# Chunk attention and two gated layers on one core: sums of x on VectorE, exponent terms on ScalarE, the low part of g taken last

## The chip, the cores and the metric

The kernel runs on one NeuronCore of a Trainium2 chip. Five engines work side by side, each through its own queue in order: TensorE (PE, matrix products; PEld is its loading of weights), VectorE (DVE), ScalarE (ACT), GpSimd (POOL) and SyncE (SP, which issues most DMAs). An instruction waits only at the head of its own queue, and all that stands behind it waits too. The metric is the device time of one execution in microseconds (us); lower is better.

## The reference

```python
# q, k, v: (4, 8, 576, 64); attention inside chunks of 64 positions
scores = q_c @ k_c.T / 8
attn = exp(scores - max); attn /= sum(attn) + 1e-9
x = (attn @ v_c)  -> (2304, 512)            # tokens x model
g = (x @ w_a) * (x @ w_b)                    # 512 -> 1536
y = g @ w_out                                # 1536 -> 512
h = y @ w_in                                 # 512 -> 2048
P = a0 + a1 h + a2 h^2 + a3 h^3
Q = 1 + |b0||h| + |b1| h^2
out = (P / (Q + 1e-6)) @ w_out2              # 2048 -> 512
```

All inputs are float32. Each matrix product is taken in three parts (high by high, high by low, low by high), so every operand is split into a rounded high part (ACT copies it) and the rest (a subtraction).

## The kernel before

The 2304 tokens are three groups of 768. The program is written in the order in which each engine is to do it; there is no scheduler behind it.

**Stage A** (up to about 197 us of the trace): attention in 18 units of 128 tokens, the first three at once (a list called FIRST), the others between the products x@w_a and x@w_b of the first group, which are taken directly (`ab_half`, 384 tokens at a time). After every six matmuls `half()` emits pieces of other work: the weights' conversion (`w_piece`, four pieces per tile: an ACT and a DVE instruction make the exponent terms, DVE shifts one, ACT writes the mantissa's low part, a DVE instruction adds them, then high and low parts) and whatever a list of due times (`todo`, moved on by `tick`) has due. A unit of attention is seven such entries (transposes of k and q, scores, exp, softmax, transpose, product with v); FROM, PER and GAP set their distances. Scores and the product with v share the PSUM buffers `a` and `b`.

**Sums of x.** For groups 1 and 2 the products use seven products of half matrices instead of eight. `x_first` and `x_second` make the sums and splits of x that this needs: 8 subtractions (L433) and 14 low parts (L415), each 128x768, all on POOL; high parts on ACT (L414). They read two x32 buffers; the next group's copies (L396) wait until a buffer is done with.

**Stage B** (about 197 to 383 us): 24 steps (`s_step`), each with products 1, 2, 5, 6, 4 of its own tile and products 7 (`third`) and 3 (`last`) of the step before. Product 3 adds into the tile q that the DVE instruction at L613 has to read first. `s_prep` makes sums and splits of the weights on DVE and ACT. In `fill()` the pieces of w_out's conversion and the due entries are emitted.

**Stage C** (about 383 to 557 us): y = g @ w_out in five blocks of tokens (256, then four of 512) and 12 tiles each, 60 steps. In each, `g_fetch` brings g back from DRAM two steps ahead, ACT makes its high part (L649), DVE its low part (L651), and `y_part` takes 4 x 3 matmuls into four accumulators, column block by column block. Between them the second layer's weights are converted; their DMAs and those of g stand in one SP queue. g_hi and g_lo have two buffers each.

**Stage D** (from about 552 us): `step2` takes h = y @ w_in, the rational function on ACT and DVE and the last product. Tile (0, 2) of h is the first that uses PSUM buffer `a`.

At the start SP issues the loads of attention and weights, then two tiny ones of the constants a and b; ACT's absolute value of b (L818) stands directly behind FIRST.

Of the kernel before, what the change touches and what calls it, by code (L numbers as in the profile page):

```python
# [15 lines left out]
ALU = mybir.AluOpType  # L16
# [4 lines left out]
def chunk_attention_two_mlps(  # L21
# [176 lines left out]
    def w_piece():  # L198


        n, piece = divmod(n_cv[1], 4)
        n_cv[1] += 1
        key = order[n]
        if piece == 0:
            w_fetch_ahead(n)
            t = raws.pop(key)

            terms[n] = (t, *w_tile(key, I32))
        t, c, z = terms[n]
        hw = t[:, :, 1]  # L210
        lw = t.rearrange("p f t -> p (f t)").bitcast(U16).rearrange("p (f t) -> p f t", t=4)[:, :, 1]
        zz = z.bitcast(F16).rearrange("p (f t) -> p f t", t=2)
        if piece == 0:
            nc.scalar.activation(zz[:, :, 1], hw.bitcast(F32), AF.Copy, scale=2.0 ** -112)
            nc.vector.tensor_scalar(c.bitcast(F32), hw.bitcast(F32), 2.0 ** -112, None, ALU.mult)
        elif piece == 1:
            w_hi(n - 1)
            nc.vector.tensor_scalar(c, c, 3, None, ALU.logical_shift_left)
        elif piece == 2:
            nc.scalar.activation(zz[:, :, 0].bitcast(U16), lw, AF.Copy, scale=2.0 ** -13)  # L220
            w_lo(n - 1)
            w_fetch_ahead(n + 1)
        else:
            del terms[n]
            x = f32s[n] = p_io.tile([P, DM], I32, name="w_x", tag="io")
            nc.vector.tensor_tensor(x, c, z, ALU.add)
            if key in w1_d:
                nc.gpsimd.dma_start(out=w1_d[key], in_=x.bitcast(F32))

    def w_until(tiles):  # L230

        while n_cv[1] < min(4 * tiles, 4 * n_cv[2]):
            w_piece()

    def w_flush():

        n = n_cv[1] // 4 - 1
        if n in f32s:
            w_hi(n)
            w_lo(n)  # L240

    def mm3(ps, w, x, first, last, **kw):
        (wh, wl), (xh, xl) = w, x
        nc.tensor.matmul(ps, wh, xh, start=first, stop=False, **kw)  # L244
        nc.tensor.matmul(ps, wh, xl, start=False, stop=False, **kw)  # L245
        nc.tensor.matmul(ps, wl, xh, start=False, stop=last, **kw)  # L246

    def cols(pair, k):
        return [t[:, k * P:(k + 1) * P] for t in pair]
# [5 lines left out]
    def later(dt, f):  # L255
        todo.append((now[0] + dt, n_todo[0], f))
        n_todo[0] += 1
# [152 lines left out]
    def x_hl(g, c, x):  # L410
        t = x_block(g, c)
        hi, lo = t[:, 0], t[:, 1]
        return (
            lambda: nc.scalar.copy(hi, x),  # L414
            lambda: nc.gpsimd.tensor_tensor(lo, x, hi.bitcast(F32), ALU.subtract),  # L415
        )

    def x_first(g):
# [7 lines left out]
    def x_second(g):  # L426


        x1, x2 = un.pop(("x32", g, 0)), un.pop(("x32", g, 1))
        b11, b21, b12, b22 = x1[:, 0:2], x1[:, 2:4], x2[:, 0:2], x2[:, 2:4]  # L430

        def sub(o, x, y):
            return lambda: nc.gpsimd.tensor_tensor(o, x, y, ALU.subtract)  # L433

        h3, l3 = x_hl(g, 3, b22)
        h5, l5 = x_hl(g, 5, b11)
        h7, l7 = x_hl(g, 7, b12)
        h6, l6 = x_hl(g, 6, b11)
        h4, l4 = x_hl(g, 4, b21)
        for at, f in (  # L440
            (0.5, sub(b11, b12, b11)), (0.5, h3), (0.5, sub(b12, b22, b12)),
            (1.5, l3), (1.5, h5), (2, h7),
            (2, l5), (2.5, sub(b11, b22, b11)),
            (3.5, l7), (3.5, h6), (4, sub(b21, b21, b11)),
            (4.5, l6), (5, h4),
            (5.5, l4),
        ):
            later(at, f)

    def a_unit(u, at, times):  # L450

# [188 lines left out]
    def g_fetch(j, i):  # L640
        t = p_io.tile([P, SIZES[j]], F32, name="g_raw", tag="io")
        nc.sync.dma_start(out=t, in_=g_d[i][:, START[j]:START[j] + SIZES[j]])
        raw["g", j, i] = t
# [7 lines left out]
        return lambda: nc.vector.tensor_tensor(lo, x, hi.bitcast(F32), ALU.subtract)  # L651

    def y_part(j, i):
        if i == 0:
            places = [(ps_acc, "acc")] * KD if j % 2 == 0 else [(ps_at, "at"), (ps_at, "at"), (ps_ab, "a"), (ps_ab, "b")]
            acc[j] = [pool.tile([P, SIZES[j]], F32, name="acc", tag=tag) for pool, tag in places]
        w, g = wt["o", i], g1.pop((j, i))
        for d in range(KD):
            mm3(acc[j][d], cols(w, d), g, i == 0, i == F1 - 1)
            if i == F1 - 1:  # L660
                evac.append(lambda d=d: y_out(j, d))

# [141 lines left out]
    for item in FIRST:  # L804
# [9 lines left out]
        else:  # L814
            {"S": a_scores, "X": a_exp, "E": a_soft, "P": a_ptrans, "V": a_pv, "L": lambda u: un.pop(("lo", u))()}[
                what
            ](u)
    nc.scalar.activation(cb_t, cb_t, AF.Abs)  # L818
    for u in (2 * UH, 2 * UH + 1):
        a_load(u, "k", "q", "v") if u == 2 * UH else a_load(u, "v")  # L820

# [1 line left out]
    seq = [(i, h) for h in range(2) for i in range(4)] + [(i, h) for i in range(4, F1) for h in range(2)]  # L823
    for n in range(UH):
        a_unit(UH + n, 1.0 + 0.5 * n, (0, 0.5, 1.5, 2, 2.5, 3.5, 4.5))
    FROM, PER, GAP = 6.0, 2.75, 1.0
    times = (0, 0.5, 2, 3, 3.5, 5, 6.5)
    for n in range((NQ - 1) * 2 * UH):
        a_unit(2 * UH + n, FROM + PER * n + (GAP if n >= 2 * UH else 0), times)
# [11 lines left out]
    def s_do(t, op):  # L841
        if op == 0:
            preps[t] = s_prep(t)
        preps[t][op]()
        if op == 11 and t + 2 < F1:
            s_load(t + 2)
# [49 lines left out]
    def fill():  # L896
        step, m = place
        place[1] += 1
        for t, op in plan.get((step, m), ()):
            s_do(t, op)  # L900
        if (step, m) == (1, 3):
            w_fetch_ahead(len(order1))
        if step >= 2 and (7 * step + m) % 3 == 0:
            w_until(min(n_cv[1] + 1, 4 * n_cv[2]) / 4)
        tick(0.5)

    for n, (i, g) in enumerate(seq2):
# [2 lines left out]
            g_fetch(0, 0)  # L910
            g_fetch(0, 1)
        prev = s_step(i, g, prev, fill)
    place[:] = [len(seq2), 2]
    s_step(None, None, prev, fill)
    tick(100.0)
    w_until(n_cv[2])
    w_flush()
    g_parts(0, 0)()
    s_t.close()
    phase.close()  # L920
    s_x32.close()
# [10 lines left out]
    done = n_cv[1]  # L932
    a_ring = None
    for n, (j, i) in enumerate(places):
        if n + 2 < len(places):
            g_fetch(*places[n + 2])
        due = done + (4 * len(order2) * spent[n] // spent[-1] if n < len(spent) else 4 * len(order2))
        due -= n_cv[1]
        low = lambda: None
        if n + 1 < len(places):  # L940
            low = g_parts(*places[n + 1])
        if due:
            w_piece()
        low()
        for _ in range(due - 1):
            w_piece()
        y_part(j, i)
        evacuate(1)
        if j == NB - 1:
            if 2 <= i < 2 + KD:  # L950
                y_split(0, i - 2)
            if 1 <= i < 1 + KD:
                y_fetch(0, i - 1)
            if i >= F1 - EARLY:
                if a_ring is None:
                    w_flush()
                    s_cv.close()
                    p_a = ctx.enter_context(tc.tile_pool(name="a", bufs=1, side="right", reuse_waits="tile"))
                    a_ring = p_a.tile([P, AN], F32, name="a_ring", tag="a_ring")
                step2(i - (F1 - EARLY))  # L960
# [32 lines left out]
```

## Time and profile before

| | |
|---|---|
| time, median of 3 runs | 960.22 us (957.68 to 961.83) |
| the profiled execution's time | 956.45 us |
| its span, first to last instruction | 954.7 us |
| PE busy | 909.1 us (95%) |
| PEld, DVE, ACT, POOL busy | 798.4, 745.0, 594.2, 107.0 us |
| granted TensorE clock, mean | 0.977 of full speed |

Matmuls are pipelined, so a busy PE need not be PE at its rate: the count of matmuls in a stretch tells more. In the rows further down a timeline row is: start, duration, engine, line, operation, output<-inputs, shape, count, and in brackets the idle time before it and what ended that. A row of stretches is: the stretch and its length, then busy time and count of each engine, the granted clock, the DMA engines' share and GB/s.

### The profile page before, as it was taken

The page shows a single profiled execution, that of the slowest core. Times are in us where ns is not written, and L with a number is a line of the kernel's source. Part 1 is how long each engine was busy: PE and PEld are TensorE (multiplying, and loading weights), DVE is VectorE, ACT ScalarE, POOL GpSimd, SP SyncE. Part 2 cuts the span into 40 slices and gives each one's busy share as a digit, 9 for nine tenths or more (in the row PEclk, how much of TensorE's full clock was granted, in tenths as well). Part 3 has the DMA queues.
Part 4 walks back from the last instruction along what each step waited for, and adds up shares of the span by engine and source line. Part 5 has one row for each costly group of instructions (what it writes and reads, how often), then busy time and mean ns, then how long its engine had stood idle before and what let it go on. Part 6 is the DMA issues. An engine that isn't in the chain of part 4 may idle for free.

```text
span 954.7 us, 14746 instructions
## 1 busy us (share of the span) xinstructions
PE 909.1 (95%) x5516; PEld 798.4 (84%) x5516; DVE 745.0 (78%) x1334; ACT 594.2 (62%) x1070; POOL 107.0 (11%) x144
## 2 busy tenths in 40 slices
PE   6779998979999999899999899999999999999998
PEld 5669987979999999777777699888888888888897
DVE  5467889596888886466666569999888988988896
ACT  4546766534445453366666568887668767776875
POOL 0111354361111111000000000000000000000000
PEclk8789999979999999899999999999999999999999
DMA  9957996224443323457676520020002002000100
GB/s 230 246 168 202 250 239 162 84 81 138 139 147 133 130 99 109 136 191 246 224 245 213 203 89 1 1 77 1 1 1 89 0 1 76 3 1 1 45 1 34
DMA packets 107335, 105.82 MB, mean 111 GB/s; under 512 B 61440, under 2 KB 84480, under 8 KB 107264
## 3 DMA queue, kind: packets, MB, share of 16 engines
q1 hardware_dynamic: 99264, 79.71, 28.6%
q0 software_dynamic: 8000, 25.17, 7.3%
q8 instruction: 43, 0.70, 0.3%
q14 instruction: 28, 0.23, 0.1%
HBM read 74.98 MB, written 29.88 MB: 110 GB/s over the span
## 4 chain that ended last, share of the span: by engine, by line
PE 74%; DMA 9%; ACT 6%; DVE 5%; SPq 4%; issue 2%; ACTq 0%; DVEq 0%
PE acc L245 8%; PE acc L246 8%; PE acc L244 8%; DMA g_raw<-g_d 7%; PE h L246 7%; PE h L244 7%; PE h L245 7%; PE ab L244 3%; PE ab L246 3%; PE ab L245 3%; PE y L246 3%; PE y L245 3%; PE y L244 3%; SPq L313 2%; PE q L244 2%
## 5 line engine op out<-in xcount | busy, mean ns | idle before, releaser
L246 PE MATMUL h<-y,w_i 128*128 128x512 f32 (+1 forms) x320 | 117.8, 368 | 0.0
L244 PE MATMUL h<-y,w_i 128*128 128x512 f32 (+1 forms) x320 | 117.8, 368 | 0.0
L245 PE MATMUL h<-y,w_i 128*128 128x512 f32 (+1 forms) x320 | 117.7, 368 | 0.0
L716 ACT ACTIVATE a_ring<-h 128x512 f32<-128x512 f32 (+1 forms) x80 | 44.1, 551 | 88.8 <-PE h L246 88.8
L245 PE MATMUL acc<-g_lo,w_o 128*128 128x512 f32 (+1 forms) x240 | 92.7, 386 | 5.4 <-DVE g_lo L651 5.0
L244 PE MATMUL acc<-g_hi,w_o 128*128 128x512 f32 (+1 forms) x240 | 91.7, 382 | 5.0 <-ACT g_hi L649 4.9
L572 ACT COPY s<-y 128x384 f32<-128x384 f32 x72 | 34.5, 479 | 90.5 <-PE y L246 89.3
L246 PE MATMUL acc<-g_hi,w_o 128*128 128x512 f32 (+1 forms) x240 | 90.5, 377 | 0.0
L651 DVE TENSOR_TENSOR g_lo<-g_raw,g_hi 128x512 fp32r<-128x512 f32 (+1 forms) x60 | 38.1, 637 | 54.8 <-ACT g_hi L649 54.7
L719 DVE SCALAR_TENSOR_TENSOR u<-u,cb_t,a_ring 128x512 f32<-128x512 f32 (+1 forms) x80 | 55.7, 696 | 31.3 <-ACT u L717 30.4
L245 PE MATMUL acc<-w_o,g_hi 128*128 128x512 f32 x191 | 75.2, 394 | 0.0
L244 PE MATMUL acc<-w_o,g_hi 128*128 128x512 f32 x191 | 74.8, 392 | 0.0
L246 PE MATMUL acc<-w_o,g_lo 128*128 128x512 f32 x191 | 74.2, 388 | 0.0
L649 ACT CAST g_hi<-g_raw 128x512 fp32r<-128x512 f32 (+1 forms) x60 | 34.5, 575 | 63.2 <-DMA g_raw<-g_d 45.5
L244 PEld LDWEIGHTS h<-y,w_i 128*128 128x128 f32 x320 | 60.1, 188 | 9.0
L245 PEld LDWEIGHTS h<-y,w_i 128*128 128x128 f32 x320 | 60.1, 188 | 8.7
L246 PEld LDWEIGHTS h<-y,w_i 128*128 128x128 f32 x320 | 60.0, 188 | 7.5
L486 POOL DMA_DIRECT2D g_d<-g x72 | 40.6, 565 | 203.4 <-DVE g L616 83.2
L245 PEld LDWEIGHTS acc<-g_lo,w_o 128*128 128x128 f32 x240 | 46.5, 194 | 20.1 <-DVE g_lo L651 12.1
L244 PEld LDWEIGHTS acc<-g_hi,w_o 128*128 128x128 f32 x240 | 46.5, 194 | 17.7 <-ACT g_hi L649 9.6
L718 ACT ACTIVATE t<-h,ca_t 128x512 f32<-128x512 f32 (+1 forms) x80 | 59.0, 738 | 0.0
L721 DVE SCALAR_TENSOR_TENSOR t<-t,ca_t,h 128x512 f32<-128x512 f32 (+1 forms) x80 | 55.6, 694 | 2.8
(193 smaller groups left out, 2522.6 us busy)
## 6 DMA issues: line engine op xcount, KB each, us to landing
w_raw<-in_moe_w_out_dram SPq DMA_DIRECT2D x28, 512.0 KB, 3.8
g_d<-g POOLq DMA_DIRECT2D x72, 192.0 KB, 2.4
g_raw<-g_d SPq DMA_DIRECT2D x48, 256.0 KB, 4.2
w_raw<-in_moe_w_in_dram SPq DMA_DIRECT2D x16, 512.0 KB, 4.0
w_raw<-in_moe_w_a_dram SPq DMA_DIRECT2D x12, 512.0 KB, 5.4
w_raw<-in_moe_w_b_dram SPq DMA_DIRECT2D x12, 512.0 KB, 4.8
out_dram<-o SPq DMA_DIRECT2D x18, 256.0 KB, 2.3
y_d<-ys POOLq DMA_DIRECT2D x16, 256.0 KB, 4.4
```

The costliest lines, as they stand in the source:

```text
L244: nc.tensor.matmul(ps, wh, xh, start=first, stop=False, **kw)
L245: nc.tensor.matmul(ps, wh, xl, start=False, stop=False, **kw)
L246: nc.tensor.matmul(ps, wl, xh, start=False, stop=last, **kw)
L313: nc.sync.dma_start(out=dst, in_=s.rearrange("h s d -> s h d"))
L486: nc.gpsimd.dma_start(out=g_d[i][:, tok:tok + GH], in_=g)
L572: nc.scalar.copy(t, ps)
L649: nc.scalar.copy(hi, x)
L651: return lambda: nc.vector.tensor_tensor(lo, x, hi.bitcast(F32), ALU.subtract)
L716: nc.scalar.activation(ah, ps, AF.Abs)
L718: nc.scalar.activation(t, ps, AF.Identity, scale=ca_t[:, 3:4], bias=ca_t[:, 2:3])
L719: nc.vector.scalar_tensor_tensor(u, u, cb_t[:, 0:1], ah, ALU.add, ALU.mult)
L721: nc.vector.scalar_tensor_tensor(t, t, ca_t[:, 1:2], ps, ALU.add, ALU.mult)
```

## The change

Five edits, in the order of the program:

- The constants' absolute value moves from behind FIRST to the third filler of stage B's second step.
- For tiles 8 to 35 of the weights the second exponent term is an ACT instruction instead of a DVE one (16 tiles in stage A, 12 in stage B).
- All 22 subtractions of x run on DVE. Those of `x_second` come in a new order, spread over four units of due time; for the last group they begin three units later, in stage B. PER goes from 2.75 to 2.65 and GAP from 1 to 2.
- At the end of stage B the first step of stage C is placed between products 7 and 3 of the last step; its g_hi and a third fetch of g come before product 7.
- `y_part` takes both products with g_hi of all four column blocks first, then the four with g_lo. The accumulators change buffers: two of `acc` always, and `a`, `b` for even blocks, `at`, `at` for odd ones (before: four of `acc` for even, `at`, `at`, `a`, `b` for odd).

```diff
-            nc.vector.tensor_scalar(c.bitcast(F32), hw.bitcast(F32), 2.0 ** -112, None, ALU.mult)
+            if 8 <= n < len(order1) + len(ordero):
+                nc.scalar.activation(c.bitcast(F32), hw.bitcast(F32), AF.Copy, scale=2.0 ** -112)
+            else:
+                nc.vector.tensor_scalar(c.bitcast(F32), hw.bitcast(F32), 2.0 ** -112, None, ALU.mult)
...
-            lambda: nc.gpsimd.tensor_tensor(lo, x, hi.bitcast(F32), ALU.subtract),
+            lambda: nc.vector.tensor_tensor(lo, x, hi.bitcast(F32), ALU.subtract),
...
-            return lambda: nc.gpsimd.tensor_tensor(o, x, y, ALU.subtract)
+            return lambda: nc.vector.tensor_tensor(o, x, y, ALU.subtract)
...
-        for at, f in (
-            (0.5, sub(b11, b12, b11)), (0.5, h3), (0.5, sub(b12, b22, b12)),
-            (1.5, l3), (1.5, h5), (2, h7),
-            (2, l5), (2.5, sub(b11, b22, b11)),
-            (3.5, l7), (3.5, h6), (4, sub(b21, b21, b11)),
-            (4.5, l6), (5, h4),
-            (5.5, l4),
-        ):
-            later(at, f)
+        ops = (
+            sub(b11, b12, b11), h3, sub(b12, b22, b12), h5, l3, h7, l5, sub(b11, b22, b11), sub(b21, b21, b11),
+            h6, l7, h4, l6, l4,
+        )
+        at = 0.5 if g < NQ - 1 else 3.5
+        for n, f in enumerate(ops):
+            later(at + 0.5 * (n * 9 // len(ops)), f)
...
         if i == 0:
-            places = [(ps_acc, "acc")] * KD if j % 2 == 0 else [(ps_at, "at"), (ps_at, "at"), (ps_ab, "a"), (ps_ab, "b")]
+            places = [(ps_acc, "acc")] * 2
+            places += [(ps_at, "at")] * 2 if j % 2 else [(ps_ab, "a"), (ps_ab, "b")]
...
-        w, g = wt["o", i], g1.pop((j, i))
+        w, (gh, gl) = wt["o", i], g1.pop((j, i))
         for d in range(KD):
-            mm3(acc[j][d], cols(w, d), g, i == 0, i == F1 - 1)
+            wh, wl = cols(w, d)
+            nc.tensor.matmul(acc[j][d], wh, gh, start=i == 0, stop=False)
+            nc.tensor.matmul(acc[j][d], wl, gh, start=False, stop=False)
+        for d in range(KD):
+            wh, wl = cols(w, d)
+            nc.tensor.matmul(acc[j][d], wh, gl, start=False, stop=i == F1 - 1)
...
-    nc.scalar.activation(cb_t, cb_t, AF.Abs)
...
-    FROM, PER, GAP = 6.0, 2.75, 1.0
+    FROM, PER, GAP = 6.0, 2.65, 2.0
...
+        if (step, m) == (1, 2):
+            nc.scalar.activation(cb_t, cb_t, AF.Abs)
...
-    place[:] = [len(seq2), 2]
-    s_step(None, None, prev, fill)
     tick(100.0)
     w_until(n_cv[2])
+    g_parts(0, 0)()
+    g_fetch(0, 2)
+    third, last = prev
+    third()
     w_flush()
-    g_parts(0, 0)()
+    y_part(0, 0)
+    last()
...
-        if n + 2 < len(places):
+        if 0 < n < len(places) - 2:
             g_fetch(*places[n + 2])
...
-        y_part(j, i)
+        if n:
+            y_part(j, i)
```

How the instructions stand in three places. DVE at the start of stage B, before (`ws`, `j_x` and `wf` are parts and sums of weights, `a_` and `b_` results of a step, `at`, `g` those of attention and stage A):

```order
L544 TENSOR_TENSOR ws_2665<-wf,ws_2665 128x512
L490 TENSOR_TENSOR g<-ab,a_s 128x384
L590 TENSOR_TENSOR a_2703<-x,s 128x384
L544 TENSOR_TENSOR ws_a<-wf,ws_a 128x512
L544 TENSOR_TENSOR ws_b<-wf,ws_b 128x256
L549 TENSOR_TENSOR wf<-wf 128x256 x4
L544 TENSOR_TENSOR j_x<-wf,j_x 128x512 x2
L590 TENSOR_TENSOR a_2762<-x,s 128x384
L613 TENSOR_TENSOR b_2745<-q,s 128x384
```

And now, from the same instruction on (`x_1987`, `x_2392` are the last group's x, `xs` its parts):

```order
L436 TENSOR_TENSOR x_1987<-x_2392,x_1987 128x768
L491 TENSOR_TENSOR g<-ab,a_s 128x384
L436 TENSOR_TENSOR x_2392<-x_2392 128x768
L591 TENSOR_TENSOR a_2695<-x,s 128x384
L545 TENSOR_TENSOR ws_a<-wf,ws_a 128x512
L545 TENSOR_TENSOR ws_b<-wf,ws_b 128x256
L418 TENSOR_TENSOR xs<-x_2392,xs 128x768
L550 TENSOR_TENSOR wf<-wf 128x256 x2
...
L545 TENSOR_TENSOR j_x<-wf,j_x 128x512 x2
L418 TENSOR_TENSOR xs<-x_2392,xs 128x768
L591 TENSOR_TENSOR a_2761<-x,s 128x384
L614 TENSOR_TENSOR b_2743<-q,s 128x384
```

Nine instructions of 768 columns now stand among the eleven that were there. PE at the end of stage B, before (y is product 7 of the last step, q product 3, w_o_24 the first tile of w_out):

```order
L244 MATMUL y<-xs,j_x 128x384
L245 MATMUL y<-xs,j_x 128x384
L246 MATMUL y<-xs,j_x 128x384
L244 MATMUL q<-xs,j_x 128x384
L245 MATMUL q<-xs,j_x 128x384
L246 MATMUL q<-xs,j_x 128x384
L244 MATMUL acc<-g_hi,w_o_24_3003 128x256
L245 MATMUL acc<-g_lo,w_o_24_3003 128x256
L246 MATMUL acc<-g_hi,w_o_24_3003 128x256
```

And now:

```order
L249 MATMUL y<-xs,j_x 128x384
L663 MATMUL acc<-g_hi,w_o_24_3003 128x256
L664 MATMUL acc<-g_hi,w_o_24_3003 128x256
L667 MATMUL acc<-g_lo,w_o_24_3003 128x256 x4
L247 MATMUL q<-xs,j_x 128x384
L248 MATMUL q<-xs,j_x 128x384
L249 MATMUL q<-xs,j_x 128x384
L663 MATMUL acc<-g_hi,w_o_25_3136 128x256
```

The first step of stage C has gone between the two products, its four products with g_lo at its end. PE at the start of stage D, now (w_i_1 and w_i_2 are tiles 1 and 2 of w_in; what an instruction waits for stands in brackets):

```order
L247 MATMUL h<-y,w_i_1_38_4820 128x384
L248 MATMUL h<-y,w_i_1_38_4820 128x384
L249 MATMUL h<-y,w_i_1_38_4820 128x384
L247 MATMUL h<-y,w_i_2_40_4912 128x384 [waits Activation_49]
L248 MATMUL h<-y,w_i_2_40_4912 128x384
```

Before, the first matmul of tile 2 carried no wait; now it waits for an ACT instruction, since its buffer `a` belongs to the last block's accumulators.

## Rows read from the trace of the kernel before

**Rows 1.** Busy time, counts and clock by stretch; PE's count comes first.

```profile
140.00:160.00 20.00, 15.17 (x167) 13.46 (x165) 19.76 (x27) 9.61 (x19) 12.38 (x11) 0.91 0.66 168
160.00:180.00 20.00, 20.00 (x234) 18.45 (x232) 16.49 (x35) 14.46 (x28) 7.00 (x9) 1.00 0.47 136
200.00:220.00 20.00, 15.51 (x62) 14.80 (x63) 16.33 (x20) 6.88 (x13) 7.67 (x6) 0.74 0.34 105
240.00:260.00 20.00, 20.00 (x117) 20.00 (x116) 16.92 (x35) 9.08 (x19) 3.24 (x6) 1.00 0.41 139
420.00:540.00 120.00, 115.62 (x476) 87.57 (x474) 78.18 (x144) 77.03 (x132) 6.49 (x13) 1.00 0.71 238
640.00:760.00 120.00, 120.00 (x529) 99.05 (x528) 106.91 (x163) 87.01 (x144) 0.00 (x0) 1.00 0.05 18
```

**Rows 2.** Timeline at the start, about the constants' absolute value.

```profile
31.39 0.43 SPq L800 DMA_DIRECT2D cb_t<-in_moe_b_dram  x1
...
36.28 0.20 ACT L818 ACTIVATE cb_t<-cb_t 128x2 f32<-128x2 f32 x1 [8.80 <-DMA cb_t<-in_moe_b_dram]
...
38.00 1.11 PE L322 MATMUL at<-ident,kqv 128*128 128x128 f32 x4 [5.03 <-ACT kT L324]
...
39.94 0.80 ACT L214 ACTIVATE w_a<-w_raw 128x512 f16<-128x512 f32 x1
```

**Rows 3.** Groups of one line and form: count, busy us, mean ns of one.

```profile
L415 POOL TENSOR_TENSOR xs<-x,xs 128x768 fp32r<-128x768 f32 x14 | 26.1, 1869 | 1.3 <-ACT xs L414 1.2
...
L214 ACT ACTIVATE w_o<-w_raw 128x512 f16<-128x512 f32 x28 | 22.2, 792 | 0.3 <-DMA w_raw<-in_moe_w_out_dram 0.3
...
L196 DVE TENSOR_TENSOR w_o<-w_x,w_o 128x512 fp32r<-128x512 f32 x28 | 19.2, 685 | 0.3
...
L616 DVE TENSOR_TENSOR g<-g,a 128x384 f32<-128x384 f32 x24 | 13.4, 558 | 0.8
...
L215 DVE TENSOR_SCALAR w_o<-w_raw 128x512 f32<-128x512 f32 x28 | 11.8, 421 | 0.3 <-DMA w_raw<-in_moe_w_out_dram 0.3
```

**Rows 4.** Timeline in stage A, while POOL makes the sums.

```profile
144.30 5.43 DVE L359 TENSOR_SCALAR s<-s 128x8 f32<-128x8 f32 x1
...
146.19 0.65 ACT L396 COPY x<-at 128x256 f32<-128x256 f32 x2 [6.20 <-POOL xs L415]
...
146.62 1.40 PE L339 MATMUL at<-kT,qT 64*64 64x64 f32 x32 [4.32 <-ACT x L396]
```

**Rows 5.** Timeline of PE in the first two steps of stage B.

```profile
202.16 0.69 PE L244 MATMUL q<-xs,ws 128*128 128x384 f32 x1 [3.16 <-ACT ws L540]
...
211.09 0.44 PE L246 MATMUL y<-xs,ws_a 128*128 128x384 f32 x1 [2.33 <-DVE ws_a L544]
```

**Rows 6.** Timeline from stage B to stage C.

```profile
382.20 0.55 DVE L615 TENSOR_TENSOR g<-r,s 128x384 f32<-128x384 f32 x1
382.34 0.44 PE L244 MATMUL q<-xs,j_x 128*128 128x384 f32 x1 [1.16 <-DVE b L613]
...
385.83 0.58 PE L245 MATMUL acc<-g_lo,w_o 128*128 128x256 f32 x1 [2.06 <-DVE g_lo L651]
...
390.07 0.28 PE L244 MATMUL acc<-g_hi,w_o 128*128 128x256 f32 x1
390.19 0.28 PE L245 MATMUL acc<-g_lo,w_o 128*128 128x256 f32 x1
```

**Rows 7.** Who waited for whom, 405 to 545 us: total, times, longest.

```profile
ACT g_hi L649 <- DMA g_raw<-g_d: 42.4, 28, 2.5
...
PEld acc L245 <- DVE g_lo L651: 9.5, 22, 0.8
...
ACT g_hi L649 <- PE acc L246: 2.3, 5, 0.9
```

**Rows 8.** Timeline at the start of stage D.

```profile
559.41 0.33 PE L244 MATMUL h<-y,w_i 128*128 128x384 f32 x1
...
561.42 1.58 ACT L665 COPY ys<-acc 128x512 f32<-128x512 f32 x3
```

## The prediction

> **What bounds the kernel now.** I read the busy shares first: PE 95%, DVE 78%, ACT 62%, POOL 11%. So TensorE sets the pace, and time can be won only where it stands still, runs at a lower granted clock, or gets its operands late. A busy share hides the last of these, so next I read the stretches with their counts of matmuls [rows 1]. 640 to 760 us in stage D is PE at its rate: 529 matmuls in 120 us, nothing to gain. Three stretches fall short of an equal one: 140 to 160 us (167 matmuls against 234), 200 to 220 us (62 against 117) and stage C (476 against 529, with PE called 96% busy). For each I then read the timeline for who was waited for [rows 2, 4 to 6, 8], and for stage C the table of waits [rows 7]. The sum below is against the profiled execution, 956.45 us (span 954.7 and 1.75 around it); the median 960.22 lies 3.8 above it, and the forecast is put on the median's basis at the end.
>
> **The change part by part.**
>
> *Absolute value moved.* ACT waits 8.80 us for the tiny DMA of b; the copy of kT stands behind it, and PE waits 5.03 us for that copy [rows 2]. Both go. What is late next: ACT's L214 on tile w_a_4, whose DMA stands right behind b's in SP's queue. It is issued no earlier than 31.39 + 0.43 = 31.82; with b's own 4.9 us from issue to use it is there at 36.7, a third longer 38.3. Before, ACT came to it at 39.94 without waiting, so at the worst only 39.94 - 38.3 = 1.6 us come back; at the best the 5.03 and some clock, 6.2. PE has products of its own ahead of what w_a_4 makes, so I take the value near its wait: -4.5. Moved to stage B, the instruction costs 0.20 us on an ACT that is under half busy there (9.08 of 20 us [rows 1]): 0. If that cover were gone it would cost its 0.2.
>
> *Sums of group 1, stage A.* 167 matmuls instead of 234 in 20 us are (67/234) x 20 = 5.7 us. Their cause stands in the timeline: a DVE instruction on 8 elements takes 5.43 us while POOL makes a sum, and ACT's copy L396 waits 6.20 us for POOL's low part, PE 4.32 for the copy [rows 4]. With the sums on DVE both go. No row has a DVE sum of 768 columns. From below: 558 ns for 384 and 685 for 512 columns [rows 3] are 127 ns per 128, so 685 + 2 x 127 = 0.94 us. From above: POOL's 1.87 us for the same tile. I take 0.94, as its two rows are of the same engine and operation. Nine of the 11 sums of a group fall close together: 9 x 0.94 = 8.5 us, in some 12 us in which DVE is otherwise about 80% taken (16.49 of 20), less what the moved exponent terms free (0.42 each, against 0.79 on ACT [rows 3]). That leaves a backlog of 3 to 5 us on DVE; before, DVE at 19.76 of 20 stopped PE through POOL's stretching alone. GAP and PER also put three scores right behind a product with V, which share PSUM buffers through an ACT copy of 0.65 us [rows 4]: some 2 us in all. So 5.7 - 2 = -3.7; bounds -5.7 (all back) and +3 (the backlog shows whole while most of the old loss stays gone).
>
> By the Trainium skill, "SBUF — State Buffer", section "Summary: rules for kernel authors", a DVE instruction with two SBUF inputs and a GpSimd one that reads SBUF exclude each other, and the second to issue is blocked until the first is done. The 5.43 us for 8 elements bear that out as far as one row can; by that rule the stretching ends with POOL's last sum, and the last rival below is what it would be without it.
>
> *Start of stage B.* 55 of 117 matmuls are missing in 200 to 220 us, 9.4 us, and the wait of 3.16 us that ended at 202.16 began 1.0 before 200 [rows 1, 5]: 10.4 us lost. Named waits are 3.16 + 2.33 = 5.5; the rest is a granted clock of 0.74. Cause: POOL's eight subtractions and low parts are finished late and DVE runs slowly beside them, so ws and ws_a are late. Now nine sums stand among DVE's eleven instructions: 9 x 0.94 + 4 x 0.558 + 3 x 0.685 + four of 256 columns at 0.43 (the 558 less 127) = 14.5 us, ending in b (L614), with half a us for the start 15.0. PE has 11 products of 6 matmuls of 20/117 = 0.171 us before it needs b's buffer, 11.3 us. So about 3.5 us of the loss return as a new wait on b: 10.4 - 3.5 = -6.9. Bounds: -9 (parts of that row of sums start before stage B), -2.6 (the wait costs as much in clock as the old one: 3.5 x 10.4/5.5 = 6.6, and another 1.2 of late start).
>
> *Stage B to C.* PE waits 1.16 us for b (L613) and 2.06 for g_lo, then runs slowly: from 385.83 to 390.07 there are 23 matmuls, 0.184 us each, and 0.12 from there on (390.07 to 390.19) [rows 6], some 23 x 0.07 = 1.6. Together 4.8. Now product 3's waiting is covered by 12 matmuls of y. Left are the accumulator whose buffer L615 (now L616) frees, about 0.9, and g_lo behind its ACT copy, about 0.65 (a copy of that size [rows 4]): 1.55. So -3.3; bounds -4.6 and -1.0 (the two waits come one after the other and the clock falls again).
>
> *Low part last, stage C.* (529 - 476)/529 x 120 = 12 us are lost in that stretch. The weight loads wait 9.5 us in 22 cases for g_lo, which the new order first needs seven matmuls later [rows 7]. But ACT's g_hi waits 42.4 us in 28 cases for g's DMA, and only 2.3 in 5 for PE to free a buffer [rows 7]: data, not PE, come late. The fetch of g stands in SP's queue behind the weights' DMAs, which wait for ACT to free their buffers, and ACT stands behind g_hi. A later need of g_lo leaves this loop as long as it is, and PE then waits for g_hi instead. I take -2.0, a fifth of the 9.5; bounds 0 and -9.5.
>
> *Accumulators in other buffers, stage D.* The last block's third accumulator now lies in `a`, which h tile (0, 2) needs. PE came to that tile at 559.41; the three copies L665 that empty the accumulators began at 561.42 and took 0.53 each, so the second ended at 562.47 [rows 8]. That is a new wait of 3.1 us at the head of PE's queue, with all of stage D behind it, and stage D is at PE's rate and gives nothing back. Lower clock follows a wait: 0.9 us per us waited at 200 us (10.4 against 5.5), 0.3 at 140 us (5.7 against 4.32); 0.6 of 3.1 is 1.9. So +5.0; bounds +3.1 and +6.
>
> *w_out's twelve exponent terms on ACT* lie in stage B beside an ACT under half busy [rows 1]: 0; without that cover 12 x 0.79.
>
> Sum: -4.5 - 3.7 - 6.9 - 3.3 - 2.0 + 5.0 = -15.4, so 941.0 for the profiled execution and about 945 by the median.
>
> **The rivals.**
>
> *The g_lo waits return in full.* For it: 22 waits with that name, 9.5 us. Against it: the 42.4 us for the DMA. The sum has 7.5 more: 937.5.
>
> *ACT becomes the bound in stage A.* 16 terms of 0.79 us come to an ACT at 14.46 of 20 us [rows 1, 3]; at one per 5 us it is 17.6. PE waits there for ACT's copies already [rows 4]. If half of 16 x 0.79 = 12.7 us shows, 6.3 is lost: about 951. Against it: the terms sit between pieces and not at the head of a copy PE is late for.
>
> The Trainium skill, "ScalarE: Activation LUTs", section "Rules for kernel authors", says that multiplying and adding belong on VectorE, which speaks against this edit; 421 ns on DVE against 792 on ACT agree. Whether it costs time hangs on the slack of ACT alone.
>
> *A DVE sum costs what POOL's does (the slower side).* At 1.87 us each, nine sums more than fill DVE in two places, in stage A and at the start of stage B: 2 x 9 x 0.93 = 16.8 us more, 962. The gain is gone where a sum costs 0.94 + 15.4/18 = 1.8 us. Against it: 558 and 685 ns for the same operation.
>
> *It doesn't do what it says: the stretching isn't POOL's.* Then a long DVE instruction stays long and both places keep their loss: 3.7 + 6.9 = 10.6 less gain, 955.6. For it: DVE shows two-input instructions everywhere. Against it: an 8-element instruction of 5.43 us with POOL alone at work beside it.
>
> **How the numbers follow.** The forecast 0.50, g_lo in full 0.20, ACT the bound 0.17, no stretching by POOL 0.08, dear sums 0.05. 0.5% (4.8 us, below 955.4 or above 965.0) is about what a measurement of this kernel can tell from no change. Faster: 0.48 + 0.20 + 0.13 + 0.04 = 0.85; within: 0.02 + 0.04 + 0.04 + 0.01 = 0.11; slower: 0.04, all from dear sums. The bounds added up would be 928 to 964. The range 936 to 955 holds the forecast with its usual spread, g_lo in full down to a little below its own time, and most of ACT as the bound; it leaves out the dear sums, half of the no-stretching case and the far end of g_lo's, about 0.2.
>
> **What the new profile would show.** ACT has no long wait near 31 us and PE none for kT of 5 us. POOL has no tensor instruction, and DVE's small instructions in stage A are short again. The stretch 200 to 220 us has about 95 to 100 matmuls, with a wait on b of 2 to 4 us. Between products 7 and 3 of the last step stand 12 matmuls of y. In stage C the waits on g_lo nearly vanish, and those for g_hi on PE rise. At h tile (0, 2) PE waits some 3 us for ACT, with a low clock behind it. The forecast is wrong if sums take over 1.2 us, if the wait in stage D is missing (then some 5 us faster), if PE waits for ACT in stage A more than before, or if g_hi is no longer late in stage C.

## The result, and the profile after

The changed kernel takes 945.16 us (median of 4 runs, 944.55 to 946.14) against 960.79 (957.68 to 961.83): ratio 0.9844, interval 0.9819 to 0.9869. The forecast was 945, range 936 to 955. The two profiled executions differ by less: 946.14 is the highest of the new kernel's four, 956.45 lies under all four timed runs of before, and their difference is 10.3 us where the medians' is 15.6. The sum was laid against the profiled execution, 956.45 - 15.4 = 941.0, and there 946.14 was measured, 5.1 more; that the median met the forecast so closely is luck, as the end of the term-by-term section shows. To size the terms, note in both traces when PE starts the same matmul of the program. The places used here are:

| PE starts | before | after | gain so far | gain since |
|---|---|---|---|---|
| a sixth of group 1's products | 71.3 | 69.7 | 1.5 | 1.5 |
| stage B | 196.7 | 189.8 | 7.0 | 5.4 |
| a twelfth of stage B | 221.6 | 207.0 | 14.7 | 7.7 |
| a twelfth of stage C | 394.0 | 376.9 | 17.1 | 2.4 |
| the last matmul of stage C | 557.1 | 541.9 | 15.1 | -2.0 |
| a quarter of h | 632.5 | 622.2 | 10.3 | -4.8 |

From there on both run alike. The last column answers to the six terms of the sum (forecast: 4.5, 3.7, 6.9, 3.3, 2.0, -5.0).

Busy time, counts and clock by stretch of the changed kernel, columns as in [rows 1]:

```profile
140.00:160.00 20.00, 19.76 (x288) 17.75 (x278) 17.61 (x38) 16.57 (x34) 4.14 (x8) 1.00 0.80 213
200.00:220.00 20.00, 19.20 (x108) 18.57 (x108) 15.39 (x30) 9.08 (x20) 2.92 (x5) 1.00 0.45 155
420.00:540.00 120.00, 113.34 (x470) 87.72 (x469) 74.34 (x137) 73.08 (x127) 6.48 (x12) 0.99 0.65 215
640.00:760.00 120.00, 120.00 (x529) 99.10 (x528) 106.64 (x161) 87.01 (x144) 0.00 (x0) 1.00 0.05 18
```

The holes at 140 and at 200 us are closed (288 and 108 matmuls; 167 and 62 before), at a granted clock of 1.00, TensorE's upper level of 2.4 GHz; shares between 0.5 and 1 are means of time there and at the lower level, 1.2 GHz. Stage C is no better: 470 matmuls, 476 before.

The timeline at the start, answering to [rows 2]:

```profile
30.79 0.48 ACT L877 COPY a_s<-ab 128x384 f32<-128x384 f32 x1 [3.81 <-PE ab L249]
...
37.83 0.78 ACT L214 ACTIVATE w_a<-w_raw 128x512 f16<-128x512 f32 x1 [3.12 <-DMA w_raw<-in_moe_w_a_dram]
...
39.09 0.66 PE L325 MATMUL at<-ident,kqv 128*128 128x128 f32 x4 [1.45 <-ACT qT L327]
```

The wait for b's DMA is gone; the one for w_a_4's, next in the queue, has come in its place, and PE waits 1.45 us behind it. The sums of x as groups (count, busy us, mean ns), answering to the first row of [rows 3]:

```profile
L418 DVE TENSOR_TENSOR xs<-x,xs 128x768 fp32r<-128x768 f32 x14 | 13.1, 948 | 0.0
...
L436 DVE TENSOR_TENSOR x<-x,x 128x768 f32<-128x768 f32 x4 | 3.8, 950 | 0.0
```

PE's waits at the start of stage B and between B and C, from the timeline, answering to [rows 5, 6]:

```profile
199.77 0.44 PE L249 MATMUL q<-xs,j_x 128*128 128x384 f32 x1 [1.13 <-DVE j_x L545]
...
203.91 0.44 PE L247 MATMUL q<-xs,ws 128*128 128x384 f32 x1 [0.74 <-DVE b L614]
...
368.80 0.39 PE L663 MATMUL acc<-g_hi,w_o 128*128 128x256 f32 x1 [1.59 <-DVE g L616]
...
372.39 0.72 PE L667 MATMUL acc<-g_lo,w_o 128*128 128x256 f32 x4 [0.64 <-DVE g_lo L652]
```

Who waited for whom in stage C (388 to 530 us), answering to [rows 7]:

```profile
ACT g_hi L650 <- DMA g_raw<-g_d: 43.8, 27, 3.3
...
PE acc L663 <- ACT g_hi L650: 10.2, 14, 2.1
```

PE has no wait for g_lo left there; PE's own waits for g_hi, 2.9 us before, are 10.2. The start of stage D, answering to [rows 8]:

```profile
546.28 1.58 ACT L673 COPY ys<-acc 128x512 f32<-128x512 f32 x3
...
547.42 0.45 PE L247 MATMUL h<-y,w_i 128*128 128x384 f32 x1 [2.99 <-ACT ys L673]
```

That is the forecast new wait, at its place and with its size.

### The profile page after: what moved, and what is told of

Its sections match the earlier page's. It is cut to its first block, busy times and chain, and to the rows that moved or that the text cites. A ratio compares the mean times of both kernels' runs of the same rounds, so it can differ in the third digit from the quotient of the medians.

```text
span 944.4 us, 14722 instructions
## 1 busy us (share of the span) xinstructions
PE 901.9 (95%) x5516; PEld 793.1 (84%) x5516; DVE 725.4 (77%) x1328; ACT 607.0 (64%) x1098; POOL 64.3 (7%) x122
## 4 chain that ended last, share of the span: by engine, by line
PE 52%; issue 24%; DMA 7%; ACT 5%; DVE 4%; SPq 4%; POOL 3%; POOLq 0%; ACTq 0%; DVEq 0%
PE h L247 7%; PE h L249 7%; PE acc L248 7%; PE h L248 7%; PE acc L247 7%; PE acc L249 7%; DMA g_raw<-g_d 6%; POOL g_d L487 3%; SPq L316 2%; PE ab L247 2%; PE ab L249 2%; PE ab L248 2%; ACT g_hi L650 1%; SPq L169 1%; PE acc L663 1%
## 5 line engine op out<-in xcount | busy, mean ns | idle before, releaser
L663 PE MATMUL acc<-g_hi,w_o 128*128 128x512 f32 (+1 forms) x240 | 90.2, 383 | 14.1 <-ACT g_hi L650 12.4
L664 PE MATMUL acc<-g_hi,w_o 128*128 128x512 f32 (+1 forms) x240 | 87.9, 373 | 0.0
L667 PE MATMUL acc<-g_lo,w_o 128*128 128x512 f32 (+1 forms) x240 | 60.9, 376 | 0.6 <-DVE g_lo L652 0.6
L737 DVE SCALAR_TENSOR_TENSOR u<-u,r 128x512 f32<-128x512 f32 (+1 forms) x80 | 50.5, 631 | 9.1 <-ACT r L736 9.1
L736 ACT ACTIVATE r<-r,nlsh 128x512 f32<-128x512 f32 (+1 forms) x80 | 54.6, 682 | 2.6
```

Source lines behind the costliest of these rows:

```text
L663: nc.tensor.matmul(acc[j][d], wh, gh, start=i == 0, stop=False)
L664: nc.tensor.matmul(acc[j][d], wl, gh, start=False, stop=False)
L667: nc.tensor.matmul(acc[j][d], wh, gl, start=False, stop=i == F1 - 1)
L736: nc.scalar.activation(r, r, AF.Exp, scale=-1.0, bias=nlsh[:, 1:2])
L737: nc.vector.scalar_tensor_tensor(u, u, 1.0 + 1e-6, r, ALU.add, ALU.mult)
```

## The experiments

Each kernel is the changed one with the edit that its diff or its text shows. Numbers per place are how much later (+) or earlier (-) PE is than in the changed kernel's trace at the places of the table above. Traces of the same code differ too: seven of them lie between 68.3 and 70.4 at 70 us, and from a twelfth of stage C to its end, where the changed kernel takes 165.0 us, the traces with the same code there take 161.9 (experiment 10) to 167.7 (experiment 7). The kernel before was timed beside each group of kernels, and its five medians lie between 960.3 and 961.9: a difference of 1 to 2 us between medians shows nothing.

**1. The sums back on POOL.**

```diff
-            lambda: nc.vector.tensor_tensor(lo, x, hi.bitcast(F32), ALU.subtract),
+            lambda: nc.gpsimd.tensor_tensor(lo, x, hi.bitcast(F32), ALU.subtract),
...
-            return lambda: nc.vector.tensor_tensor(o, x, y, ALU.subtract)
+            return lambda: nc.gpsimd.tensor_tensor(o, x, y, ALU.subtract)
```

> The changed kernel with its 22 subtractions of x (sums and low parts) back on POOL, in the new order and at the new due times. Theory: the engine is what gained in stage A and at the start of stage B, 6.0 and 7.7 us in the two traces; with POOL the 8-element DVE instructions of stage A are long again (over 2 us, not 0.17), few matmuls run near 140 to 160 us (under 200) and at the start of stage B (under 80 in 20 us), and the time is 954 to 962. Rival: the new order and due times are what gained, not the engine; then at most 3 us are lost, 944 to 948.

961.83 us, ratio to before 1.0001 (0.9983 to 1.0018): with this one edit undone nothing of the whole change is left. By place: -0.7 at 70 us, +7.5 at the start of stage B, +16.6 a twelfth into it, +15.8 at the end. With the new order the engine is worth 8.2 us in stage A and 9.2 at the start of stage B; experiment 8 has the old order. The timeline of DVE and POOL in stage A:

```profile
142.81 1.82 POOL L418 TENSOR_TENSOR xs<-x,xs 128x768 fp32r<-128x768 f32 x1
...
142.94 6.10 DVE L221 TENSOR_SCALAR w_b<-w_b 128x512 int32<-128x512 int32 x1 [3.81 <-ACT w_b L216]
...
144.56 0.56 POOL L487 DMA_DIRECT2D g_d<-g  x1
145.15 3.60 POOL L418 TENSOR_TENSOR xs<-x,xs 128x768 fp32r<-128x768 f32 x2
```

and the stretches of the same kernel:

```profile
140.00:160.00 20.00, 14.37 (x181) 12.64 (x171) 15.07 (x22) 13.84 (x26) 10.51 (x11) 0.83 0.55 146
200.00:220.00 20.00, 11.62 (x49) 10.48 (x48) 18.28 (x15) 7.06 (x15) 15.55 (x10) 0.74 0.28 84
```

A shift of 512 columns starts 0.13 us after a POOL subtraction and ends at 149.04, 0.29 us after POOL's third one (148.75). One of the 18 instructions on 8 elements takes 2.15 us again. The same shift takes 0.41 us in the changed kernel:

```profile
142.59 0.41 DVE L221 TENSOR_SCALAR w_b<-w_b 128x512 int32<-128x512 int32 x1
```

The rule of the Trainium skill that the prediction drew on ("SBUF — State Buffer", section "Summary: rules for kernel authors") agrees with these rows in part: the instruction that came second is blocked. But the rule ends the block with the first instruction, and the shift was held through three. And the prediction took the rule's case of two SBUF inputs, while the shift, like the 8-element instruction of [rows 4], reads a single tensor; the rule names a 2-port perf mode of DVE as its other case, and no run here shows in which mode these instructions ran.

Near 200 us only 49 matmuls run. The theory held; the rival, that the engine gained nothing, fell.

**2. Copies ahead of stage D.**

```diff
-        evacuate(1)
+        evacuate(KD if (j, i) == (NB - 1, F1 - 1) else 1)
```

> The changed kernel with the last block's four accumulators all copied out directly behind its last product, ahead of ACT's work on the first tiles of h. Theory: the 2.99 us wait of PE at h tile (0, 2) and the slow clock behind it cost 4.8 us that nothing gives back; here the second copy ends near 542.8, before PE comes to the tile (544.4), the wait is gone and the time is 4 to 5 lower, 940 to 941. Rival: stage D is also bound by ACT's chain on h (the copies delay it by 1.6 us), PE waits at the last product instead and the time stays within 1.5 of 945.

944.13 us (941.46 to 944.93), 1.0 under the changed kernel: by the median the rival's time, while the profiled execution, the 941.46, shows the theory's mechanism. By place it is +0.2 at the end of stage C and -4.7 a quarter into h. The copies, and the first matmul of h tile (0, 2), which waited:

```profile
541.83 2.06 ACT L673 COPY ys<-acc 128x512 f32<-128x512 f32 x4 [0.57 <-PE acc L667]
...
544.42 0.33 PE L247 MATMUL h<-y,w_i 128*128 128x384 f32 x1
```

All four copies end at 543.89, before PE comes to the tile; the wait has gone, and its 4.8 us with it. The median alone would not have shown it; the trace of experiment 12 shows it again.

**3. Loads of g in POOL's queue.**

```diff
-        nc.sync.dma_start(out=t, in_=g_d[i][:, START[j]:START[j] + SIZES[j]])
+        nc.gpsimd.dma_start(out=t, in_=g_d[i][:, START[j]:START[j] + SIZES[j]])
```

> The changed kernel with the loads of g in stage C issued by POOL's queue, where they no longer stand behind the weights' loads in SP's. Theory: the loop g_hi, ACT's last read of a weight's raw tile, SP's next load of weights, SP's load of g, g_hi sets the pace of stage C; without it ACT's 43.8 us of waits for g's DMA fall below 15, PE's 10.2 us of waits for g_hi below 3, and the time is 6 to 12 lower, 933 to 939. Rival: DMA bandwidth and ACT's own work set the pace, or the other queue's loads land later: the waits keep their size and the time is within 2 of 945, or higher.

943.22 us; stage C's end at -0.2. As it stands the theory missed. Its table of waits, 388 to 530 us:

```profile
ACT g_hi L650 <- DMA g_raw<-g_d: 27.0, 13, 4.1
ACT g_hi L650 <- PE acc L664: 12.4, 15, 1.5
```

and POOL's timeline at a change of block:

```profile
418.78 0.76 POOL L643 DMA_DIRECT2D g_raw<-g_d  x1 [2.38 <-DVE w_o L196]
428.51 0.55 POOL L674 DMA_DIRECT2D y_d<-ys  x1 [8.97 <-ACT ys L673]
429.05 0.55 POOL L643 DMA_DIRECT2D g_raw<-g_d  x1
```

Inside a block ACT now waits for PE, as the theory has it. At a change of block the loads of g stand behind y's stores, which wait for the accumulators, and PE is no earlier at the end of the stage. That calls for experiment 5.

**4. Products with g_lo inside, as before.**

```diff
         for d in range(KD):
-            wh, wl = cols(w, d)
-            nc.tensor.matmul(acc[j][d], wh, gh, start=i == 0, stop=False)
...
+            mm3(acc[j][d], cols(w, d), g, i == 0, i == F1 - 1)
```

> The changed kernel with the products of stage C in the old order, g_lo second of each three. Theory: the loads of g set the pace, so the waits on g_lo (9.5 us in 22 cases) return and those on g_hi shrink by about as much; stage C itself is no longer (within 1.5), but product 3 at the end of stage B covers less of the wait for the first g_lo (1 to 2): 945 to 948. Rival: the g_lo waits were a loss of their own: 9 to 10 slower, 954.

946.77 us, as the theory said. From a twelfth of stage C to its end it takes 165.7 us, the changed kernel 165.0, before 163.0: no difference beyond the scatter. The waits of the weight loads from 388 to 530 us come back on g_lo and shrink on g_hi, 18.4 us in the changed kernel:

```profile
PEld acc L248 <- DVE g_lo L652: 11.0, 25, 0.8
PEld acc L247 <- ACT g_hi L650: 9.3, 14, 1.9
```

Between a late place of stage B (eleven twelfths of it) and the first twelfth of C it is 3.0 us slower than the changed kernel. The wait that returns there:

```profile
373.06 0.39 PE L248 MATMUL acc<-g_lo,w_o 128*128 128x256 f32 x1 [1.38 <-DVE g_lo L652]
```

**5. Two queues.**

```diff
-        nc.sync.dma_start(out=t, in_=g_d[i][:, START[j]:START[j] + SIZES[j]])
+        (nc.gpsimd if j else nc.sync).dma_start(out=t, in_=g_d[i][:, START[j]:START[j] + SIZES[j]])
...
-        nc.gpsimd.dma_start(out=y_d[:, d, START[j]:START[j] + SIZES[j]], in_=ys)
+        nc.sync.dma_start(out=y_d[:, d, START[j]:START[j] + SIZES[j]], in_=ys)
```

> The changed kernel with stage C's loads of g from the second block on issued by POOL's queue, and the stores of y by SP's, so that the loads of g stand behind nothing else. Theory: the last study's kernel freed the loads of g inside a block (ACT then waited 15 times for PE) but put them behind the stores of y at each change of block (8.97 us of POOL's wait there); without either, ACT's waits for g's DMA after the first block fall below 10 us, PE's for g_hi below 3, and stage C is 5 to 8 us shorter: 937 to 940. Rival: the pace is that of ACT or of DMA bandwidth, and stage C stays within 2 of its 175.6 us.

935.6 us (932.11 to 937.47), ratio to before 0.9732 (0.9709 to 0.9754), a little under the theory's 937 to 940. Stage C ends 9.5 us earlier; up to its start the trace is the changed kernel's to 0.1 us. Waits from 400 to 525 us (the changed kernel's there: 37.6 us of ACT for the DMA, 7.7 of PE for g_hi):

```profile
ACT g_hi L650 <- PE acc L664: 14.5, 16, 1.9
ACT g_hi L650 <- DMA g_raw<-g_d: 10.0, 9, 2.0
...
PE acc L663 <- ACT g_hi L650: 1.2, 2, 0.7
```

and the stretch, 507 matmuls where the changed kernel has 459:

```profile
400.00:520.00 120.00, 118.67 (x507) 94.73 (x506) 84.05 (x155) 83.56 (x141) 24.59 (x43) 1.00 0.75 244
```

The changed kernel has ACT busy for 76.1 us, DVE for 76.9 and a DMA share of 0.68 there. All three are higher now, so none of them was the bound: the loads of g stood behind the weights' loads. What those waited for in the changed kernel's SP queue, 388 to 530 us, is the buffers that ACT and DVE free:

```profile
SPq L169 <- ACT w_o L223: 33.6, 13, 4.5
SPq L169 <- ACT w_i L223: 26.1, 13, 4.1
```

**6. Exponent terms on DVE.**

```diff
-            if 8 <= n < len(order1) + len(ordero):
+            if False:
```

> The changed kernel with the second exponent term of tiles 8 to 35 on DVE again. Theory: DVE has its sums of group 1 between about 120 and 160 us beside 0.42 us more per tile, and falls behind there: 1 to 4 us lost in stage A, nothing in stage B, 946 to 949. Rival one: DVE has room for both, the time is the same within 1. Rival two: ACT was the bound, and stage A gets shorter by 1 to 3.

945.42 us: the same, rival one. Its trace is 3.1 us earlier at 70 us, though; PE's waits are alike there, and the stretch shows the clock (the changed kernel's below it):

```profile
56.00:70.00 14.00, 10.84 (x149) 9.80 (x148) 6.15 (x16) 4.57 (x13) 1.62 (x3) 1.00 0.47 143
```

```profile
56.00:70.00 14.00, 10.84 (x104) 9.63 (x104) 4.28 (x10) 4.74 (x12) 1.08 (x2) 0.74 0.43 128
```

The same 10.84 us of busy PE are 149 matmuls at clock 1.00 and 104 at 0.74. At 56 us the two traces are 0.1 us apart, at 67 us 3.1. In the other six traces with the changed kernel's code up to there the clock of this stretch is 0.72 to 0.88. From 140 to the end of stage A this kernel loses 0.7 us again: that is all that DVE's load costs.

**7. Terms of tiles 4 to 7 on ACT too.** `8 <= n` becomes `4 <= n`.

> The changed kernel with the second exponent term of tiles 4 to 7 on ACT as well. Theory: most of what the earlier kT gave was taken back because DVE has no idle time from 40.1 to 56.3 us; four terms of 0.42 us less there are 1 to 1.7 us, kept through stage A: 943.5 to 944.5, the first product after 70 us 1 to 1.7 earlier. Rival: the weights' loads and attention's chain of waits set the pace there: no change at 70 us (within 0.7).

948.71 us, +1.0 at 70 us: no gain, the theory missed. In this execution w_a_4's data came later, at 38.86:

```profile
38.86 0.77 ACT L214 ACTIVATE w_a<-w_raw 128x512 f16<-128x512 f32 x1 [4.62 <-DMA w_raw<-in_moe_w_a_dram]
```

and among PE's waits (us in total, times, longest):

```profile
PE at L325 <- ACT qT L327: 4.0, 1, 4.0
```

PE waits 4.0 us behind that (1.45 in the changed kernel) and is 1.9 us later there than the changed kernel. By 70 us it has won back 1.0 of that; experiments 2 and 3, which lack this edit, win back 1.4 and 0.6 from a like delay. So nothing here speaks for DVE's lack of idle time from 40 to 56 us as what took the gain back. A further 2.6 us arise in stage C and are not explained.

**8. Sums on DVE in the old order and at the old times.** `x_second`'s list, PER and GAP as before.

> The changed kernel with the sums of x on DVE but in the old order and at the old due times, also of attention's units. Theory: the engine is nearly all of the gain, the order little: within 3 of 945, the loss near 145 us not back (over 220 matmuls from 140 to 160 us). Rival: bunched in the old order and, for the last group, ahead of stage B, the sums hold up DVE's short instructions for the scores and PE waits 4 to 8 us more in stage A: 949 to 953.

949.74 us, +4.0 at the start of stage B: the rival's price. 140 to 160 us has 184 matmuls, not over 220, with a wait of 2.14 us for ACT's copy of x:

```profile
140.00:160.00 20.00, 17.86 (x184) 16.47 (x184) 16.11 (x32) 12.93 (x26) 3.23 (x6) 0.91 0.74 194
...
144.24 1.20 PE L342 MATMUL at<-kT,qT 64*64 64x64 f32 x32 [2.14 <-ACT x L399]
```

So with the sums on DVE, order and due times are worth 4.1 us in stage A, and cost 1.2 at the start of stage B. Four traces together show how the two parts of that edit work in stage A, from 70 us to the start of stage B: 125.5 us before, 128.2 with the new order on POOL (experiment 1), 124.2 with the old order on DVE, 120.1 with both (the exponent terms, the other edit in that stretch, are worth 0.4: experiment 6). Neither part alone gains more than 1.3 us there. At the start of stage B the engine is all of it: 24.9 and 26.4 us with POOL, 16.0 and 17.2 with DVE.

**9. Absolute value early.** The instruction goes back behind FIRST.

> The changed kernel with the constants' absolute value at its old place, behind the first units. Theory: PE waits 5 us again at 33 to 38 us, but most of it is hidden by what comes next (the load of w_a_4 and the first group's chain of attention, then a lower clock), so that at the first products after 70 us only 1 to 2 us are left: 946 to 947. Rival, the prediction's own term: 4.5 us stay lost to the end, 949 to 950.

948.86 us, 3.7 above the changed kernel; +7.4 soon after the wait, +3.1 at 70 us, +2.9 at the end. PE's wait in this execution:

```profile
PE at L325 <- ACT kT L327: 7.9, 1, 7.9
```

Between theory (1 to 2) and rival (4.5). The two traces with the early value are at 71.3 and 72.8 us at the first place; the seven that share the changed kernel's code up to there lie between 68.3 and 70.4. The edit is worth about 3 us; by the ratios to the kernel before, 0.9868 against 0.9844, it is 2.3, which their intervals (0.003 each) do not tell from zero.

**10. Product 3 before stage C.** The lines `y_part(0, 0)` and `last()` change places.

> The changed kernel with product 3 of stage B's last step ahead of the first step of stage C, as before, all else as changed (g_lo last too). Theory: PE waits for b (about 1.2 us) and then for the buffer of the first accumulators, 1.5 to 2.5 us more between stage B and C: 946.5 to 948. Rival: taking g_lo last covers the transition alone, within 0.7 of 945.

944.09 us (941.0 to 949.18), 1.1 under the changed kernel: 0.2 outside the rival's range, far from the theory's. From the late place of stage B to a twelfth of C it takes 23.4 us; the changed kernel takes 24.3, and eight traces with the changed kernel's code there 24.2 to 25.9. PE waits once:

```profile
366.53 0.44 PE L247 MATMUL q<-xs,j_x 128*128 128x384 f32 x1 [1.22 <-DVE b L614]
```

1.22 us here, 1.59 and 0.64 with the overlap. The rest of stage C is 3.1 us shorter in this execution with the same code; that is not claimed as an effect.

**11. Constants' loads late.** The two loads go behind those of attention's units.

> The changed kernel with the two tiny loads of the constants issued behind the loads of attention's units, so that w_a_4's load goes out about 1.5 us earlier. Theory: that load (ACT waits 3.12 us for it until 37.83) is what is late next where the constants' wait is gone; ACT waits 1 to 2 us less, PE does not wait 1.45 us at 39.09, and 1 to 1.5 us are left after 70 us: 943.5 to 944. Rival: the first group's chain of attention and DVE set the pace from 40 to 70 us, as seven runs' marks near 70 us (66.7 to 70.7) let it look; ACT waits less but nothing is left at 70 us: 944.5 to 946.

943.59 us; -2.5 at 70 us. ACT gets w_a_4 sooner (37.83 in the changed kernel):

```profile
36.99 0.78 ACT L214 ACTIVATE w_a<-w_raw 128x512 f16<-128x512 f32 x1 [2.82 <-DMA w_raw<-in_moe_w_a_dram]
```

PE's wait for qT does not follow (1.7 us), and the clock from 30 to 44 us is 1.00 instead of 0.91. The time is in the theory's range, its mechanism not shown by this trace alone.

**12. Three together** (edits 2, 5 and 11).

> The changed kernel with three of the edits above: stage C's loads of g and stores of y on two queues, the last accumulators copied out first, the constants' loads late. Theory: they lie in three stages, each bound by PE between them, so that their gains add: two queues 9.5, copies 4.7, constants 1 to 2 (less sure); 935.6 less 4.7 less 1 is 930, range 927 to 932. Rival: the block's earlier end in stage C meets the same wait for the copies elsewhere (ACT is fuller then) and the copies' gain is not had: 934 to 936.

927.8 us (925.24 to 930.27), ratio to before 0.9644 (0.9617 to 0.9671): 17.4 us under the changed kernel, inside the theory's range. In the trace -4.1 at the start of stage B, a further 9.4 by the end of stage C, a further 4.9 by a quarter of h, 18.4 in all; so the copies' gain, which the medians of experiment 2 left open, is had here. The wait for qT is 0.7 us, with w_a_4 at 35.94:

```profile
PE at L325 <- ACT qT L327: 0.7, 1, 0.7
```

## Why the prediction was right, term by term

**Sums, stage A (3.7 forecast, 5.4 in the traces).** Right in the price of a sum, 948 ns against 0.94 us, and in part in the cause: with the sums on DVE at the old times only 1.3 us come back (experiment 8). The size was too small because 2 us of loss were put down to DVE's backlog, GAP and PER. After 70 us PE waited 0.46 and 0.24 us in stage A, and the new order and times do not cost but save 4.1 us.

**Start of stage B (6.9; 7.7).** Right in cause. The waits on DVE's chain are 1.13 and 0.74 us. At the product that needs b's buffer PE is 2.7 us later than at its rate (66 matmuls of 0.173 us from 189.77 on), where 3.5 were forecast, and the clock from 200 to 220 us is 1.00, so no slow stretch follows. The longer of the waits is on j_x, not on b, and b's is shorter than the 2 to 4 us that the new profile was to show; with that, 108 matmuls run and not 95 to 100. DVE took up the sums at 190.49 us, 0.7 after stage B began, and did not pause until b was made at 203.85: 14.1 us from the start of the stage, 15.0 forecast.

**Absolute value (4.5; 1.5 in the pair of traces, about 3 by experiment 9).** What is late next was named rightly, w_a_4's load; it came at 37.83, inside the 36.7 to 38.3 of the forecast, and at 38.86 in experiment 7. The value taken was too near the whole wait. The step that failed is "PE has products of its own ahead of what w_a_4 makes". Up to 88 us PE does the same matmuls in the same order in both kernels, and the gain can be followed: 5.9 us behind the old wait, 4.4 behind the wait of 1.45 for the copy that stands behind w_a_4's tile, 3.1 behind the wait of 1.09 for DVE's e, still 3.1 at 56 us, and 1.5 at 70. The last loss comes with the clock from 56 to 70 us, 0.81 before and 0.74 in the changed kernel's trace. The row of before, to be laid beside the changed kernel's in experiment 6 (104 matmuls):

```profile
56.00:70.00 14.00, 10.84 (x136) 9.42 (x135) 7.21 (x17) 6.23 (x14) 1.70 (x3) 0.81 0.44 137
```

**Stage B to C (3.3; 2.4).** The size is near, the cause wrong. The step that failed: "product 3's waiting is covered by 12 matmuls of y". In four traces, the time from the last twelfth of stage B to a twelfth of stage C is 26.7 us with neither edit, 27.3 with the overlap alone (experiment 4), 23.4 with g_lo last alone (experiment 10), 24.3 with both (24.2 to 25.9 in eight traces). Taking g_lo last is the gain; the overlap trades a wait of 1.2 us for 1.6 (0.9 forecast) and 0.6, and no gain of its own is to be seen.

**Low part last, stage C (2.0; -2.0).** The mechanism held: the waits on g_lo turned into waits on g_hi, and nothing was gained. With one execution each, the loss of 2 us is inside the scatter of stage C; experiment 4 gives 0.6. Zero, the lower bound, would have been the better value. The loop that the prediction named (weights' loads ahead of g's in one queue) is shown by experiment 5, which takes g's loads out of it and gains 9.5 us.

**New wait, stage D (-5.0; -4.8).** Right in place, in the wait (2.99 us against 3.1) and in the clock behind it.

**Rivals.** The g_lo waits did not return in time (experiment 4). ACT is not the bound in stage A: terms on DVE or on ACT, the time is the same (experiment 6). The dear sums are excluded by 948 ns, and experiment 1 excludes that the stretching isn't POOL's. The 5.43 us row bears out a block by POOL, but not the case of two SBUF inputs: that instruction reads one tensor, and it lasts through three of POOL's, from 144.34 to 149.70:

```profile
144.34 1.81 POOL L415 TENSOR_TENSOR xs<-x,xs 128x768 fp32r<-128x768 f32 x1
146.10 1.81 POOL L433 TENSOR_TENSOR x<-x 128x768 f32<-128x768 f32 x1
147.87 1.83 POOL L415 TENSOR_TENSOR xs<-x,xs 128x768 fp32r<-128x768 f32 x1
```

Against the pair of traces the sum was 5.1 us too high (15.4 for 10.3): 3.0 too much for the absolute value, 4.0 for stage C and 0.9 for the transition, less 1.7, 0.8 and 0.2 too little for the others, each rounded. That the medians nevertheless differ by the forecast lies in which executions were profiled, a quick one of before and a slow one of the new kernel: luck, and not a sum that was right to 0.2 us. Where their 5 us lie is not shown; the clock early in stage A is one place where executions differ, by 3 us between the traces of the changed kernel and of experiment 6.

## What to carry to other kernels

Where a short VectorE instruction takes microseconds, look for a GpSimd instruction that it starts and ends with, before looking at its own size. A wait that moves from one operand to the next in the same step shows a pace set elsewhere: follow the queue of the DMA that the first of them waits for, and give urgent loads a queue in which nothing ahead of them waits. Before a buffer is given to another use, find the next user in program order and the moment at which the last reader lets it go; one such slip in a stage at its rate cost 4.8 us here, and a one-line reordering gave it back.

## What the runs showed of the hardware that was not expected

One VectorE instruction was held through three POOL subtractions in a row, 6.10 us in experiment 1 and 5.43 in the kernel before; in experiment 1 it did not get in between them, though POOL issued a DMA between the first and the second (144.56 us). Loads of g issued by POOL's queue landed about as fast as SP's: medians of 4.0 us (experiment 3) and 4.3 (experiment 5), 46 loads each, against 4.2 for SP's 47 in the changed kernel, all from 388 to 530 us.
